# Decode attention: the probabilities of two token steps as one set of 64 weight columns

## The chip, the cores and the metric

The kernel runs on one core of a Trainium2 chip. The metric is device time in microseconds (us) for one launch, as the median of three runs. Beside these runs there is one profiled execution, from which all times of single instructions, waits and transfers come.

The core has five engines, each working through its own list of instructions in order: PE (TensorE, matrix products; its weight loads are listed apart as PEld), DVE (VectorE), ACT (ScalarE), POOL (GpSimd) and SP (SyncE, which here only issues transfers). Engines wait for each other on semaphores. Transfers between device memory and the core's memory are carried by 16 DMA engines.

## The reference

One decode step (one new token for each of four sequences) of a transformer block with sliding-window attention over a cache, and then a gated MLP:

```python
x = A_x                                        # (4, 1, 576)
q = (layernorm(x) @ wq)                        # 32 heads of 128
k, v = last 4096 rows of k_cache, v_cache      # 16 heads of 128; each serves two query heads
p = softmax(q @ k.T * 128 ** -0.5)
h = x + (p @ v) @ wo
g = layernorm(h) @ W_gate
out = h + (g * (g > 0) * (layernorm(h) @ W_up)) @ W_down
```

The caches hold 16384 rows for each head, of which the window takes the last 4096. Keys and values in the window come to 4 sequences x 16 heads x 4096 x 128 bfloat16, for each of the two.

## The kernel before

**Work units.** Four key heads of one sequence form a quad: 128 partitions hold the 4096 rows of four heads (32 partitions for each head, 128 rows in each). There are 16 quads (`NQUAD`), four for each sequence, each with 4 MB of keys and 4 MB of values.

**Transfers.** SP issues all big transfers in one list (line 254 and the lambdas that it calls, L223 for keys, L228 for values, L242 to L254 for the other weights). The order is wq, K0, K1, V0, K2, V1, K3 and so on, V15, then wo, W_gate, W_up and W_down. Keys and values go round four slots of one buffer (`pool`). A transfer into a slot waits until the slot's last user is done: after keys this is the last of the four transposes of the quad (`TR`), after values the quad's last value product (`PV`). SP takes its list strictly in order. W_down waits for `ATTN`, the output projection of attention, since it overwrites the place of wo.

**One quad.** DVE transposes the keys in four parts (`tr`, L397) into three buffers; PE multiplies each part by the queries (`qk`, L463 and L465, 32 products of 512 columns, the second of each two with the weights that the first has loaded: `held`); DVE takes the maximum (`rmax`, L400), ACT and POOL bring it across the partitions, DVE makes a bias from it (`fbias`), ACT takes the exponential (L338), and DVE transposes the probabilities (`trp`, L410) into one of four buffers `pT`. PE then multiplies the values by them (`pv`). PE's order is: the key products of quad i, then the value products of quad i - 1 (`VLEAD` = 1).

**Value products.** A partition holds 128 rows of the window, as four quarters of 32 steps. For one quad `pT` holds 32 steps of 32 columns: the probabilities of the four quarters' rows at that step, for eight query heads each. One product takes the 32 columns of a step as weights and 512 moving columns, the values of the four quarters' rows at the same step, side by side. So there are 32 products in a quad, each with a weight load of its own, and they accumulate. Of each output row only the quarter of the columns is wanted whose values belong to the row's own quarter. The products of quad r of a sequence go to partitions 32r to 32r + 31 of one PSUM bank, so that the four quads of a sequence fill it; two banks (`PVB`, 4 and 5) take turns by sequence.

**Own quarter.** When a sequence is complete, `own(b)` on DVE multiplies the bank by a mask of four (`mask4`) into `own_sb` (L413), and sums over the four quarters into `acc` (L416). `ext(b)` on PE gathers the 32 heads by a 0/1 matrix (`gath`). `own` for the first three sequences runs behind the first key transpose of a later quad (i % 4 == 1); the last one runs after the loop, on the way to the output.

**End.** After the last value products come `SUM` (row sums, from `rowsum`, which DVE makes at L433), `EXT`, `NORM` (L438), `OSEL`, `ATTN` (64 products), the second layernorm, `N1` and `N2` (copies of the transposed rows, on ACT and on DVE at L444), the gate products, the up products, `HH`, two transposes (L450), the down products, one for each piece of W_down and output part, and the store.

Of the kernel before, what the change touches and what calls it, by code (L numbers as in the profile page):

```python
# [6 lines left out]
ACT = mybir.ActivationFunctionType  # L7
ALU = mybir.AluOpType
AX = mybir.AxisListType
# [93 lines left out]
def bass_sequential_preLN__sliding_block_cached__glu_gated_reglu__decode_kernel(  # L103
# [12 lines left out]
    with ExitStack() as es:  # L116
# [23 lines left out]
        own_sb = sb("own_sb", [128, 512], FP32)  # L140
        acc = sb("acc", [128, 2, DH], FP32)
        o_bf = sb("o_bf", [H, DH, B], BF16)
        mask4 = sb("mask4", [128, 4], FP32)
        gath = sb("gath", [128, H], FP32)
# [31 lines left out]
        pb += [es.enter_context(nc.psum_tensor(f"pb{i}", [128, 512], FP32))[:, :] for i in range(4, 8)]  # L176
        PVB, OB, TPB = 4, 6, 7
# [94 lines left out]
        def prog_pool(S):  # L272
            g = "gpsimd"
            S.op(g, lambda e: e.memset(eps_c[:, :], EPS), name="EPS")
            S.op(g, lambda e: e.memset(ident_b[:, :], 0.0), name="P0")
            S.op(g, lambda e: e.memset(qz[:, :, :, :, :].rearrange("p a r c m -> p (a r c m)"), 0.0), name="QZ0")
            S.op(g, lambda e: e.affine_select(out=ident_b[:, :], in_=ident_b[:, :], pattern=[[-1, 128]],  # L277
                                              compare_op=ALU.not_equal, fill=1.0, base=0, channel_multiplier=1),
                 deps=["P0"], name="IDB")
            S.op(g, lambda e: e.memset(xnT[:, :, :], 0.0), name="XNZ")  # L280
            S.op(g, lambda e: e.memset(xn4[:, :, :], 0.0), name="XN4Z")
            S.op(g, lambda e: e.memset(ones_f[:, :], 1.0), name="ONES")
            S.op(g, lambda e: e.memset(spread[:, :, :, :], 0.0), name="SP0")
            S.op(g, lambda e: e.memset(hnT[:, :, :], 0.0), name="HNZ")
            S.op(g, lambda e: e.memset(hn4[:, :, :], 0.0), name="HN4Z")
            S.op(g, lambda e: e.memset(ident_f[:, :], 0.0), name="P1")
            S.op(g, lambda e: e.affine_select(out=ident_f[:, :], in_=ident_f[:, :], pattern=[[-1, 128]],
                                              compare_op=ALU.not_equal, fill=1.0, base=0, channel_multiplier=1),
                 deps=["P1"], name="IDF")
            for i in range(NQUAD):  # L290
                deps = [("EMAX", i)]
                S.op(g, lambda e, i=i: e.partition_all_reduce(bcm[:, i % 2, :], pmax[:, i % 2, :], 128, bass_isa.ReduceOp.max),  # L292
                     deps=deps, name=("PAR", i))


        def prog_act(S):
# [9 lines left out]
            S.op(a, lambda e: e.copy(out=xnT[:, :, 0:B], in_=tpv[:, 0:16].rearrange("p (c b) -> p c b", b=B)), deps=["XNZ"], name="D_XNT")  # L306
            for u in range(2):
# [42 lines left out]
            S.op(a, lambda e: e.copy(out=hnT[0:64, 4, 0:B], in_=tpv[0:64, 16:20]), deps=["TP2", "HN4Z"], name="N1")  # L350
            for u in range(2):
# [8 lines left out]
        def prog_dve(S):  # L360
# [7 lines left out]
            def rows_norm(st, dst, src, deps, name):  # L368
# [11 lines left out]
            S.op(v, lambda e: e.tensor_scalar(out=mask[:, 1, :], in0=mask[:, 0, :], scalar1=FAR, scalar2=-FAR, op0=ALU.mult, op1=ALU.add),  # L380
                 deps=["M0"], name="M1")
            S.op(v, lambda e: e.tensor_reduce(out=mask4[:, :], in_=bass.AP(tensor=ident_b, offset=0, ap=[[128, 128], [NHQ, 4], [32, NPB], [1, NHQ]]),
                                              axis=AX.XY, op=ALU.add), name="MASK4")
            S.op(v, lambda e: e.tensor_scalar(out=foe[:, :].rearrange("p (a s x) -> p a s x", s=NS, x=2),
                                              in0=bass.AP(tensor=ident_b, offset=0, ap=[[128, NS], [0, 16], [1, NS], [0, 2]]),
                                              scalar1=FAR, scalar2=-FAR, op0=ALU.mult, op1=ALU.add), name="FOE")
# [25 lines left out]
            def own(b):  # L412
                S.op(v, lambda e: e.tensor_tensor(out=own_sb[:, :].rearrange("p (q d) -> p q d", d=DH), in0=pb[PVB + b % 2].rearrange("p (q d) -> p q d", d=DH),  # L413
                                                  in1=bass.AP(tensor=mask4, offset=0, ap=[[4, 128], [1, 4], [0, DH]]), op=ALU.mult),
                     deps=[("PV", NPB * b + NPB - 1), "MASK4"], name=("OWN", b))
                S.op(v, lambda e: e.tensor_reduce(out=acc[:, b % 2, :], in_=own_sb[:, :].rearrange("p (q d) -> p d q", d=DH), axis=AX.X, op=ALU.add),  # L416
                     deps=[("OWN", b)] + ([("EXT", b - 2)] if b >= 2 else []), name=("ACC", b))

            for i in range(NQUAD):
                for j in range(4):  # L420
                    tr(i, j)
                    if i == 0 and j == 0:
                        S.op(v, lambda e: e.transpose(out=qT[:, :], in_=q_bf[:, :, :].rearrange("p k x -> p (k x)")), deps=["QBF1"], name="D_QT")  # L423
                        S.op(v, lambda e: e.tensor_reduce(out=gath[:, :].rearrange("p (r h) -> p r h", h=NHQ),
                                                          in_=bass.AP(tensor=ident_f, offset=0, ap=[[128, 128], [32, NPB], [1, NHQ], [NHQ, 4]]),
                                                          axis=AX.X, op=ALU.add), deps=["IDF"], name="GATH")
                    if j == 0 and i > NPB and i % NPB == VLEAD:
                        own(i // NPB - 1)
# [4 lines left out]
            S.op(v, lambda e: e.tensor_tensor(out=rowsum[:, :, :].rearrange("p b (m h) -> p (b m) h", h=NHQ),  # L433
                                              in0=bass.AP(tensor=mask, offset=0, ap=[[2 * NHQ, 128], [0, NQUAD], [1, NHQ]]),
                                              in1=bass.AP(tensor=rs1, offset=0, ap=[[NQUAD, 128], [1, NQUAD], [0, NHQ]]), op=ALU.mult), name="RSUM")
            own(B - 1)
# [3 lines left out]
                 deps=["RS", ("EXT", B - 1)], name="NORM")  # L440
# [3 lines left out]
            S.op(v, lambda e: e.tensor_copy(out=hnT[:, 0:4, 0:B], in_=tpv[:, 0:16].rearrange("p (c b) -> p c b", b=B)), deps=["N1", "HN4Z"], name="N2")  # L444
# [11 lines left out]
        def prog_pe(S):  # L456
# [55 lines left out]
            def pv(i):  # L512
                b, r = divmod(i, NPB)
# [3 lines left out]
                if r == 0 and b >= 2:  # L517
                    deps.append(("OWN", b - 2))
                for t_ in range(TQ // 4):
                    last = t_ == TQ // 4 - 1  # L520
                    mm(pb[PVB + b % 2][32 * r:32 * r + 32, :].rearrange("p (q d) -> p q d", q=4), pT[i % NPT][:, 32 * t_:32 * t_ + 32],
                       vv[:, t_, :, :], t_ == 0, last, deps=deps, name=("PV", i) if last else None)
                    deps = []

            def ext(b):
                mm(pb[OB][0:H, b * DH:(b + 1) * DH], gath[:, :], acc[:, b % 2, :], True, True, deps=[("ACC", b), "GATH"], name=("EXT", b))

            for i in range(NQUAD + VLEAD):
# [3 lines left out]
                if i >= VLEAD:  # L532
                    j = i - VLEAD
                    if j % NPB == 0 and j >= NPB:
                        ext(j // NPB - 1)
# [3 lines left out]
            ext(B - 1)  # L539
# [90 lines left out]
```

## Time and profile before

| what | value |
|---|---|
| median of the runs | 379.45 us (379.43 to 379.69, 3 runs) |
| the profiled execution's own time | 379.33 us |
| span in its profile, first to last instruction | 378.0 us |
| busy: PE, DVE, ACT, POOL | 295.9, 206.0, 52.8, 11.6 us |
| read from device memory | 159.58 MB |
| granted TensorE clock, mean | 0.91 of full |

The profile page gives busy time by engine, a strip of the span in 40 slices, the DMA queues with packets and bytes, the chain of work that ended last followed back from the last instruction, and the costliest groups of instructions with what ended the idle time ahead of each. A line such as L463 is that of the helper that records matmuls, so the tile names and shapes tell which product it is (`pb<-pool,probT ... 128x512` are the value products, `sc<-kT,qz` the key products). Other views of the same trace list instructions in order of time, one row for a run of equal ones, and sum engines over chosen windows.

### The profile page before, as it was taken

Reading aid. Unit: us, or ns where it says so; the run is one execution under the profiler, and the core shown is the slowest. Engines: PE = TensorE matmul, PEld = TensorE weight load, DVE = VectorE, ACT = ScalarE, POOL = GpSimd, SP = SyncE. Lnnn points to the kernel's source line nnn. Section 1 sums busy time; section 2 is a strip of 40 time slices with the busy share of each in tenths; the row PEclk is TensorE's granted clock in tenths of the full one; section 3 lists DMA queues with packets and bytes.
Section 4 is the critical chain, followed back from the end, with each engine's and each line's share of the span. In section 5 each row is a group of like instructions: output and inputs, shape, how many; then the busy total and the mean of one; then the engine's idle time right before and its main releaser. Section 6 shows DMA issues by size and latency. Waiting matters only on the chain.

```text
span 378.0 us, 2813 instructions
## 1 busy us (share of the span) xinstructions
PE 295.9 (78%) x1392; PEld 88.3 (23%) x988; DVE 206.0 (54%) x165; ACT 52.8 (14%) x135; POOL 11.6 (3%) x32
## 2 busy tenths in 40 slices
PE   0059299999986989696959996969698969868566
PEld 0011023223131313131312231313122212322113
DVE  1237577595839392938384846565666566131130
ACT  1013402112020202020201120202002100110020
POOL 4100000000000000000000000000000000000000
PEclk9996879999996999898978998989789998989768
DMA  8999999999999999999999999999999999999995
GB/s 333 430 444 433 413 430 442 437 426 419 434 437 437 418 430 440 433 435 416 433 440 430 432 423 437 433 433 418 433 440 433 428 423 437 426 437 431 407 422 219
DMA packets 6651, 159.76 MB, mean 423 GB/s; under 512 B 744, under 2 KB 880, under 8 KB 1776
## 3 DMA queue, kind: packets, MB, share of 16 engines
q1 hardware_dynamic: 6632, 159.59, 98.6%
q8 instruction: 9, 0.15, 0.2%
q10 hardware_dynamic: 8, 0.00, 0.0%
q14 instruction: 2, 0.02, 0.0%
HBM read 159.58 MB, written 0.00 MB: 422 GB/s over the span
## 4 chain that ended last, share of the span: by engine, by line
DMA 66%; DVE 20%; PE 10%; ACT 2%; SPq 1%; issue 0%; POOL 0%; DVEq 0%
DMA pool<-in_A_k_cache_dram 52%; DVE kT L397 18%; DMA pool<-in_A_v_cache_dram 8%; DMA pool<-in_B_W_down_dram 7%; PE sc L463 4%; PE sc L465 4%; PE pb L463 2%; DVE probT L410 1%; DVE rmx L400 1%; ACT P L338 1%; SPq L254 0%; DVE o_bf L438 0%; ACT L338 0%; ACT qz L327 0%; DVE qT L423 0%
## 5 line engine op out<-in xcount | busy, mean ns | idle before, releaser
L397 DVE STREAM_TRANSPOSE kT<-pool 128x2048 f32<-128x2048 f32 x64 | 142.7, 2281 | 38.4 <-DMA pool<-in_A_k_cache_dram 37.1
L463 PE MATMUL sc<-kT,qz 128*128 128x512 bf16 x256 | 110.7, 432 | 41.2 <-DVE kT L397 41.0
L463 PE MATMUL pb<-pool,probT 128*32 128x512 bf16 (+2 forms) x584 | 120.5, 374 | 4.5 <-DVE probT L450 2.3
L465 PE MATMUL sc<-kT,qz 128*128 128x512 bf16 x256 | 110.2, 431 | 0.0
L463 PEld LDWEIGHTS pb<-pool,probT 128*32 128x32 bf16 (+1 forms) x584 | 52.8, 97 | 74.1 <-issue 13.1
L463 PEld LDWEIGHTS sc<-kT,qz 128*128 128x128 bf16 x256 | 26.7, 104 | 151.8 <-issue 74.6
L400 DVE TENSOR_REDUCE rmx<-sc 128x1 f32<-128x1024 f32 x16 | 19.6, 1224 | 38.9 <-PE sc L465 38.9
L333 ACT ACTIVATE pmax<-mask,rmx 128x8 f32<-128x8 f32 x16 | 4.8, 300 | 236.6 <-DVE rmx L400 236.6
L410 DVE STREAM_TRANSPOSE probT<-P 128x1024 bf16<-128x1024 bf16 x16 | 19.9, 1245 | 20.7 <-ACT P L338 20.7
L338 ACT ACTIVATE P<-sc,bias 128x1024 bf16<-128x1024 f32 x16 | 17.8, 1114 | 13.3 <-DVE bias L405 13.3
L327 ACT COPY qz<-qrep 32x128 bf16<-32x128 bf16 x64 | 18.8, 294 | 0.6
L475 PE MATMUL pb<-ident_b,xn_bf 4*128 4x4 bf16 (+1 forms) x5 | 0.4, 180 | 18.8 <-DVE xn_bf L370 18.8
L292 POOL PARTITION_ALL_REDUCE bcm<-pmax x16 | 5.9, 367 | 297.1 <-ACT pmax L333 297.1
L403 DVE SCALAR_TENSOR_TENSOR t<-bcm,mask 128x8 f32<-128x8 f32 x16 | 2.7, 167 | 13.3 <-POOL bcm L292 13.3
L463 PE MATMUL sc<-pool,oX 128*4 128x288 bf16 x32 | 9.0, 314 | 0.4 <-ACT oX L347 0.4
L465 PE MATMUL sc<-pool,oX 128*4 128x288 bf16 x32 | 9.0, 313 | 0.0
L413 DVE TENSOR_TENSOR own_sb<-pb,mask 128x512 f32<-128x512 f32 x4 | 2.6, 662 | 10.2 <-PE pb L463 10.2
L374 DVE TENSOR_REDUCE sel<-ident_b 128x128 bf16<-128x512 bf16 x1 | 1.0, 1010 | 12.8 <-POOL ident_b L277 12.8
L446 DVE TENSOR_TENSOR P<-pb,P 128x396 bf16<-128x396 f32 x1 | 0.6, 574 | 13.2 <-PE pb L463 13.2
L463 PE MATMUL sc<-col,foe 4*128 4x512 bf16 x16 | 6.4, 398 | 0.7 <-ACT qrep L313 0.7
L441 DVE TENSOR_TENSOR h_row<-sc,x_bf 4x576 f32<-4x576 f32 x1 | 0.7, 746 | 10.3 <-PE sc L465 10.3
L465 PE MATMUL sc<-col,foe 4*128 4x512 bf16 x16 | 6.2, 390 | 0.0
(95 smaller groups left out, 73.4 us busy)
## 6 DMA issues: line engine op xcount, KB each, us to landing
pool<-in_A_k_cache_dram SPq DMA_DIRECT2D x16, 4096.0 KB, 29.5
pool<-in_A_v_cache_dram SPq DMA_DIRECT2D x16, 4096.0 KB, 29.3
pool<-in_A_wo_dram SPq DMA_DIRECT2D x1, 4608.0 KB, 21.3
pool<-in_B_W_gate_dram SPq DMA_DIRECT2D x1, 4608.0 KB, 22.8
pool<-in_B_W_up_dram SPq DMA_DIRECT2D x1, 4608.0 KB, 25.5
pool<-in_A_wq_dram SPq DMA_DIRECT2D x1, 4096.0 KB, 13.0
pool<-in_B_W_down_dram SPq DMA_DIRECT2D x2, 1152.0 KB, 19.4
pool<-in_B_W_down_dram SPq DMA_DIRECT2D x1, 1008.0 KB, 22.5
```

The source lines that it names most:

```text
L292: S.op(g, lambda e, i=i: e.partition_all_reduce(bcm[:, i % 2, :], pmax[:, i % 2, :], 128, bass_isa.ReduceOp.max), deps=deps, name=("PAR", i))
L327: S.op(a, lambda e, src=src, dst=dst: e.copy(out=dst, in_=src), deps=deps, name=("QZ", i) if g == 3 else None, signal=g == 3)
L333: S.op(a, lambda e, i=i: e.activation(out=pmax[:, i % 2, :], in_=mask[:, 1, :], func=ACT.Identity, bias=rmx[:, i % 2:i % 2 + 1], scale=1.0 ...
L338: S.op(a, lambda e, i=i: e.activation(out=Pb[:, (i % 2) * 1024:(i % 2 + 1) * 1024], in_=sc[:, (i % 2) * 1024:(i % 2 + 1) * 1024], func=ACT ...
L374: S.op(v, lambda e: e.tensor_reduce(out=sel[:, :, :], in_=bass.AP(tensor=ident_b, offset=0, ap=[[128, 128], [0, 4], [1, 32], [32, 4]]), ax ...
L397: S.op(v, lambda e: e.transpose(out=dst, in_=src), deps=deps, name=("TR", f))
L400: S.op(v, lambda e: e.tensor_reduce(out=rmx[:, i % 2:i % 2 + 1], in_=sc[:, (i % 2) * 1024:(i % 2 + 1) * 1024], axis=AX.X, op=ALU.max), dep ...
L403: S.op(v, lambda e: e.scalar_tensor_tensor(out=t8[:, :], in0=bcm[:, i % 2, :], scalar=-SCALE, in1=mask[:, 0, :], op0=ALU.mult, op1=ALU.mul ...
L410: S.op(v, lambda e: e.transpose(out=pT[i % NPT], in_=Pb[:, (i % 2) * 1024:(i % 2 + 1) * 1024]), deps=[("EXP", i)] + ([("PV", i - NPT)] if ...
L413: S.op(v, lambda e: e.tensor_tensor(out=own_sb[:, :].rearrange("p (q d) -> p q d", d=DH), in0=pb[PVB + b % 2].rearrange("p (q d) -> p q d" ...
L463: return e.matmul(o, lhsT=l, rhs=r, start=start, stop=stop, skip_group_check=skip)
L465: return e.add_instruction(mybir.InstMatmult(name=nc.get_next_instruction_name(), start_tensor_calc=start, stop_tensor_calc=stop, bass_ski ...
```

## The change

The value products of two neighbouring token steps share one set of weights. Weights are now 64 columns (steps t and t + 1), loaded once; the values of step t are multiplied into one bank and those of step t + 1, with the held weights, into the other. Each quad so fills 64 partitions of both banks, and two quads, not four, complete a window w. Of each output row one eighth is wanted: the own quarter, and the own step's bank. The two banks are one tensor `val` of 1024 columns, and there is no second copy of it: the first product of the next window waits for `OWN` of the last.

`own` now takes 1024 columns with a mask of eight, and runs eight times instead of four; `ext` gathers in two halves, accumulated into the same bank. Four small operations change engine: `M1` and `FOE` from DVE to ACT (in the prologue, L380 and L384 before), `RSUM` from DVE to POOL (L433 before), `N2` from DVE to ACT (L444 before). A clearing of `gath` (`G0`) is added on POOL's prologue.

```diff
--- before.py
+++ after.py
@@ -137,11 +137,11 @@
         oX = sb("oX", [128, EO, B], BF16)
-        own_sb = sb("own_sb", [128, 512], FP32)
+        own_sb = sb("own_sb", [128, 1024], FP32)
         acc = sb("acc", [128, 2, DH], FP32)
         o_bf = sb("o_bf", [H, DH, B], BF16)
-        mask4 = sb("mask4", [128, 4], FP32)
-        gath = sb("gath", [128, H], FP32)
+        mask8 = sb("mask8", [128, 8], FP32)
+        gath = sb("gath", [128, 2, H], FP32)
         qrep = sb("qrep", [128, 4, H * B], BF16)
@@ -173,8 +173,10 @@
         pb = [sc[:, i * 512:(i + 1) * 512] for i in range(4)]
-        pb += [es.enter_context(nc.psum_tensor(f"pb{i}", [128, 512], FP32))[:, :] for i in range(4, 8)]
-        PVB, OB, TPB = 4, 6, 7
+        val = es.enter_context(nc.psum_tensor("val", [128, 1024], FP32))
+        pb += [val[:, i * 512:(i + 1) * 512] for i in range(2)]
+        pb += [es.enter_context(nc.psum_tensor(f"pb{i}", [128, 512], FP32))[:, :] for i in range(6, 8)]
+        OB, TPB = 6, 7
         QB = (5, 6)
@@ -277,6 +279,7 @@
                  deps=["P0"], name="IDB")
+            S.op(g, lambda e: e.memset(gath[:, :, :], 0.0), name="G0")
             S.op(g, lambda e: e.memset(xnT[:, :, :], 0.0), name="XNZ")
@@ -291,6 +294,9 @@
                      deps=deps, name=("PAR", i))
+            S.op(g, lambda e: e.tensor_tensor(out=rowsum[:, :, :].rearrange("p b (m h) -> p (b m) h", h=NHQ),
+                                              in0=bass.AP(tensor=mask, offset=0, ap=[[2 * NHQ, 128], [0, NQUAD], [1, NHQ]]),
+                                              in1=bass.AP(tensor=rs1, offset=0, ap=[[NQUAD, 128], [1, NQUAD], [0, NHQ]]), op=ALU.mult), deps=[("EXP", NQUAD - 1)], name="RSUM")
 
@@ -304,6 +310,10 @@
             S.op(a, lambda e: e.copy(out=xnT[:, :, 0:B], in_=tpv[:, 0:16].rearrange("p (c b) -> p c b", b=B)), deps=["XNZ"], name="D_XNT")
+            S.op(a, lambda e: e.activation(out=foe[:, :].rearrange("p (a s x) -> p a s x", s=NS, x=2),
+                                           in_=bass.AP(tensor=ident_b, offset=0, ap=[[128, NS], [0, 16], [1, NS], [0, 2]]),
+                                           func=ACT.Copy, scale=FAR, bias=-FAR), name="FOE")
+            S.op(a, lambda e: e.activation(out=mask[:, 1, :], in_=mask[:, 0, :], func=ACT.Copy, scale=FAR, bias=-FAR), deps=["M0"], name="M1")
             for u in range(2):
@@ -348,6 +358,7 @@
             S.op(a, lambda e: e.copy(out=hnT[0:64, 4, 0:B], in_=tpv[0:64, 16:20]), deps=["TP2", "HN4Z"], name="N1")
+            S.op(a, lambda e: e.copy(out=hnT[:, 0:4, 0:B], in_=tpv[:, 0:16].rearrange("p (c b) -> p c b", b=B)), name="N2")
             for u in range(2):
@@ -377,13 +388,8 @@
                                               axis=AX.X, op=ALU.add), name="M0")
-            S.op(v, lambda e: e.tensor_scalar(out=mask[:, 1, :], in0=mask[:, 0, :], scalar1=FAR, scalar2=-FAR, op0=ALU.mult, op1=ALU.add),
-                 deps=["M0"], name="M1")
-            S.op(v, lambda e: e.tensor_reduce(out=mask4[:, :], in_=bass.AP(tensor=ident_b, offset=0, ap=[[128, 128], [NHQ, 4], [32, NPB], [1, NHQ]]),
-                                              axis=AX.XY, op=ALU.add), name="MASK4")
-            S.op(v, lambda e: e.tensor_scalar(out=foe[:, :].rearrange("p (a s x) -> p a s x", s=NS, x=2),
-                                              in0=bass.AP(tensor=ident_b, offset=0, ap=[[128, NS], [0, 16], [1, NS], [0, 2]]),
-                                              scalar1=FAR, scalar2=-FAR, op0=ALU.mult, op1=ALU.add), name="FOE")
+            S.op(v, lambda e: e.tensor_reduce(out=mask8[:, :], in_=bass.AP(tensor=ident_b, offset=0, ap=[[128, 128], [NHQ, 8], [64, 2], [1, NHQ]]),
+                                              axis=AX.XY, op=ALU.add), name="MASK8")
             rows_norm(st1, xn_bf, x_bf, ["A_STD"], "XN")
@@ -409,39 +415,35 @@
                      deps=[("EXP", i)] + ([("PV", i - NPT)] if i >= NPT else []), name=("TRP", i))
-            def own(b):
-                S.op(v, lambda e: e.tensor_tensor(out=own_sb[:, :].rearrange("p (q d) -> p q d", d=DH), in0=pb[PVB + b % 2].rearrange("p (q d) -> p q d", d=DH),
-                                                  in1=bass.AP(tensor=mask4, offset=0, ap=[[4, 128], [1, 4], [0, DH]]), op=ALU.mult),
-                     deps=[("PV", NPB * b + NPB - 1), "MASK4"], name=("OWN", b))
-                S.op(v, lambda e: e.tensor_reduce(out=acc[:, b % 2, :], in_=own_sb[:, :].rearrange("p (q d) -> p d q", d=DH), axis=AX.X, op=ALU.add),
-                     deps=[("OWN", b)] + ([("EXT", b - 2)] if b >= 2 else []), name=("ACC", b))
+            def own(w):
+                S.op(v, lambda e: e.tensor_tensor(out=own_sb[:, :].rearrange("p (x d) -> p x d", d=DH), in0=val[:, :].rearrange("p (x d) -> p x d", d=DH),
+                                                  in1=bass.AP(tensor=mask8, offset=0, ap=[[8, 128], [1, 8], [0, DH]]), op=ALU.mult),
+                     deps=[("PV", 2 * w + 1), "MASK8"], name=("OWN", w))
+                S.op(v, lambda e: e.tensor_reduce(out=acc[:, w % 2, :], in_=own_sb[:, :].rearrange("p (x d) -> p d x", d=DH), axis=AX.X, op=ALU.add),
+                     deps=[("OWN", w)] + ([("EXT", w - 2)] if w >= 2 else []), name=("ACC", w))
 
                         S.op(v, lambda e: e.transpose(out=qT[:, :], in_=q_bf[:, :, :].rearrange("p k x -> p (k x)")), deps=["QBF1"], name="D_QT")
-                        S.op(v, lambda e: e.tensor_reduce(out=gath[:, :].rearrange("p (r h) -> p r h", h=NHQ),
-                                                          in_=bass.AP(tensor=ident_f, offset=0, ap=[[128, 128], [32, NPB], [1, NHQ], [NHQ, 4]]),
-                                                          axis=AX.X, op=ALU.add), deps=["IDF"], name="GATH")
-                    if j == 0 and i > NPB and i % NPB == VLEAD:
-                        own(i // NPB - 1)
+                        S.op(v, lambda e: e.tensor_reduce(out=bass.AP(tensor=gath, offset=0, ap=[[2 * H, 128], [H + 16, 2], [NHQ, 2], [1, NHQ]]),
+                                                          in_=bass.AP(tensor=ident_f, offset=0, ap=[[128, 128], [0, 2], [64, 2], [1, NHQ], [NHQ, 8]]),
+                                                          axis=AX.X, op=ALU.add), deps=["IDF", "G0"], name="GATH")
+                    if j == 0 and i > 1 and i % 2 == VLEAD:
+                        own(i // 2 - 1)
                 rmax(i)
 
-            S.op(v, lambda e: e.tensor_tensor(out=rowsum[:, :, :].rearrange("p b (m h) -> p (b m) h", h=NHQ),
-                                              in0=bass.AP(tensor=mask, offset=0, ap=[[2 * NHQ, 128], [0, NQUAD], [1, NHQ]]),
-                                              in1=bass.AP(tensor=rs1, offset=0, ap=[[NQUAD, 128], [1, NQUAD], [0, NHQ]]), op=ALU.mult), name="RSUM")
-            own(B - 1)
+            own(NQUAD // 2 - 1)
             S.op(v, lambda e: e.reciprocal(out=rs_sb[:, :], in_=pb[TPB][0:H, 0:B]), deps=["SUM"], name="RS")
                                               in1=bass.AP(tensor=rs_sb, offset=0, ap=[[B, H], [1, B], [0, DH]]), op=ALU.mult),
-                 deps=["RS", ("EXT", B - 1)], name="NORM")
+                 deps=["RS", ("EXT", NQUAD // 2 - 1)], name="NORM")
             S.op(v, lambda e: e.tensor_tensor(out=h_row[:, :], in0=attn, in1=x_bf[:, :], op=ALU.add), deps=["ATTN", land("x")], name="H")
             rows_norm(st2, hn_row, h_row, ["A_STD2"], "HN")
-            S.op(v, lambda e: e.tensor_copy(out=hnT[:, 0:4, 0:B], in_=tpv[:, 0:16].rearrange("p (c b) -> p c b", b=B)), deps=["N1", "HN4Z"], name="N2")
             for k, (f0, f1) in enumerate(CUTS):
@@ -510,20 +512,22 @@
             def pv(i):
-                b, r = divmod(i, NPB)
+                w, r = divmod(i, 2)
                 x0 = at[("V", i)]
                 deps = [("TRP", i), land(("V", i))]
-                if r == 0 and b >= 2:
-                    deps.append(("OWN", b - 2))
+                if r == 0 and w >= 1:
+                    deps.append(("OWN", w - 1))
                 for t_ in range(TQ // 4):
+                    k = t_ % 2
                     last = t_ == TQ // 4 - 1
-                    mm(pb[PVB + b % 2][32 * r:32 * r + 32, :].rearrange("p (q d) -> p q d", q=4), pT[i % NPT][:, 32 * t_:32 * t_ + 32],
-                       vv[:, t_, :, :], t_ == 0, last, deps=deps, name=("PV", i) if last else None)
+                    mm(val[64 * r:64 * r + 64, 512 * k:512 * k + 512].rearrange("p (q d) -> p q d", q=4), pT[i % NPT][:, 32 * (t_ - k):32 * (t_ - k) + 64],
+                       vv[:, t_, :, :], t_ < 2, t_ >= TQ // 4 - 2, deps=deps, name=("PV", i) if last else None, held=k == 1)
                     deps = []
 
-            def ext(b):
-                mm(pb[OB][0:H, b * DH:(b + 1) * DH], gath[:, :], acc[:, b % 2, :], True, True, deps=[("ACC", b), "GATH"], name=("EXT", b))
+            def ext(w):
+                b, k = divmod(w, 2)
+                mm(pb[OB][0:H, b * DH:(b + 1) * DH], gath[:, k, :], acc[:, w % 2, :], k == 0, k == 1, deps=[("ACC", w), "GATH"], name=("EXT", w))
 
@@ -531,12 +535,12 @@
                     j = i - VLEAD
-                    if j % NPB == 0 and j >= NPB:
-                        ext(j // NPB - 1)
+                    if j % 2 == 0 and j >= 2:
+                        ext(j // 2 - 1)
                     pv(j)
                 mm(pb[TPB][0:H, b:b + 1], rowsum[:, b, :], ones_f[:, 0:1], True, True, deps=["RSUM", "ONES"] if b == 0 else [], name="SUM" if b == B - 1 else None)
-            ext(B - 1)
+            ext(NQUAD // 2 - 1)
 
```

## The prediction, made before the change was run

> **What bounds the kernel now.** I read the page first: busy time, the strip and the DMA queues.
>
> ```profile
> span 378.0 us, 2813 instructions
> ...
> PE 295.9 (78%) x1392; PEld 88.3 (23%) x988; DVE 206.0 (54%) x165; ACT 52.8 (14%) x135; POOL 11.6 (3%) x32
> ...
> DMA  8999999999999999999999999999999999999995
> ...
> q1 hardware_dynamic: 6632, 159.59, 98.6%
> q8 instruction: 9, 0.15, 0.2%
> ```
>
> The 16 DMA engines are at nine tenths or more in every slice but the first and last, and the data queue takes 98.6% of their span: the kernel moves 159.6 MB and cannot end before they are through. No compute engine passes 78%. Then I read one quad in the timeline, for how far compute stays behind the transfers.
>
> ```profile
> 132.57 8.89 DVE L397 STREAM_TRANSPOSE kT<-pool 128x2048 f32<-128x2048 f32 x4 [1.00 <-DMA pool<-in_A_k_cache_dram]
> ...
> 135.63 0.39 PE L465 MATMUL sc<-kT,qz 128*128 128x512 bf16 x1
> ...
> 135.85 0.39 PE L463 MATMUL sc<-kT,qz 128*128 128x512 bf16 x1
> ...
> 143.42 7.08 PE L463 MATMUL pb<-pool,probT 128*32 128x512 bf16 x32
> ...
> 147.21 1.25 DVE L410 STREAM_TRANSPOSE probT<-P 128x1024 bf16<-128x1024 bf16 x1 [1.27 <-ACT P L338]
> ...
> 152.00 8.89 DVE L397 STREAM_TRANSPOSE kT<-pool 128x2048 f32<-128x2048 f32 x4 [3.54 <-DMA pool<-in_A_k_cache_dram]
> ```
>
> Quads follow each other every 19.43 us (152.00 - 132.57). DVE's chain for one, first transpose to last, takes 15.9 us (147.21 + 1.25 - 132.57); then DVE waits 3.54 us for keys. From the chain of waits:
>
> ```profile
> 141.49 29.95 DMA pool<-in_A_k_cache_dram
> ...
> 258.06 29.92 DMA pool<-in_A_k_cache_dram
> ```
>
> A key transfer lands 29.95 us after its slot came free. From 171.44 (141.49 + 29.95) to 287.98 twelve transfers land, 9.71 us each. So when one is issued, about 20 us (29.95 - 9.71) of other transfers are still ahead of it: a slot may come free that much later before a DMA engine runs dry.
>
> **How the end comes about.**
>
> ```profile
> 318.72 7.08 PE L463 MATMUL pb<-pool,probT 128*32 128x512 bf16 x32
> ...
> 323.68 0.25 DVE L433 TENSOR_TENSOR rowsum<-mask,rs 128x128 f32<-128x128 f32 x1
> ...
> 326.97 6.42 PE L463 MATMUL pb<-pool,probT 128*32 128x512 bf16 x29 [1.17 <-DMA pool<-in_A_v_cache_dram]
> ...
> 334.08 0.69 DVE L413 TENSOR_TENSOR own_sb<-pb,mask 128x512 f32<-128x512 f32 x1 [10.15 <-PE pb L463]
> ...
> 334.80 1.02 DVE L416 TENSOR_REDUCE acc<-own_sb 128x128 f32<-128x512 f32 x1
> ```
>
> ```profile
> 347.98 8.89 SPq L254 DMA_DIRECT2D pool<-in_B_W_down_dram  x7
> ...
> 351.60 0.17 DVE L444 COPY hnT<-pb 128x16 bf16<-128x16 bf16 x1 [0.69 <-ACT hnT L350]
> ...
> 355.48 0.70 PE L463 MATMUL pb<-h_row,ident_f 4*4 4x320 f32 x4
> 359.64 0.52 PE L463 MATMUL pb<-pool,hnT 128*32 128x396 bf16 x4 [3.46 <-DMA pool<-in_B_W_up_dram]
> ...
> 367.81 5.00 PE L463 MATMUL pb<-pool,probT 128*4 128x320 bf16 x46 [2.32 <-DVE probT L450]
> ...
> 373.41 0.98 PE L463 MATMUL pb<-pool,probT 128*4 128x320 bf16 x12 [0.60 <-DMA pool<-in_B_W_down_dram]
> ...
> 374.78 1.37 PE L463 MATMUL pb<-pool,probT 128*4 128x320 bf16 x14 [0.40 <-DMA pool<-in_B_W_down_dram]
> ...
> 376.20 0.41 ACT L357 CAST out_sb<-pb 4x320 bf16<-4x320 f32 x1 [9.98 <-PE pb L463]
> ```
>
> The chain of the last quad waits for V15 (1.17 us), for W_up (3.46) and for pieces of W_down (0.60, 0.40); after the last piece some 2 us remain. W_down is issued at 347.98, while W_up still comes until 359.64, so there are over 11 us in the queue. The end is the landing of W_down's last piece. What makes that late is seen in narrow windows:
>
> ```profile
> 374.00:374.50 0.50, 0.38 (x6) 0.04 (x1) 0.00 (x0) 0.00 (x0) 0.00 (x0) 1.00 0.19 71
> 374.50:375.50 1.00, 0.70 (x8) 0.33 (x8) 0.00 (x0) 0.00 (x0) 0.00 (x0) 1.00 0.06 23
> ```
>
> The last column but one is the DMA share. 0.19 is three engines of 16, and 0.06 is one alone: for about 0.9 us, to nearly 375.5, fifteen DMA engines are done and one works off its part.
>
> **Part by part.** *Transfers of data*: unchanged, 0.
>
> *PE's value products.* 512 products of 512 columns stay; every second weight load goes, 256 in all. PE goes at 221 ns a product with a load each (7.08 / 32), against 220 between key products (135.85 - 135.63), where every second load is held. So the loads were hidden, and I count 0. A product with 64 weight columns is not in the trace; the neighbours, 32 and 128 columns, go at 221 and 220 ns, so I take the same.
>
> *DVE's own parts.* The rows, by line:
>
> ```profile
> L400 DVE TENSOR_REDUCE rmx<-sc 128x1 f32<-128x1024 f32 x16 | 19.6, 1224 | 38.9 <-PE sc L465 38.9
> ...
> L405 DVE TENSOR_REDUCE bias<-t 128x1 f32<-128x8 f32 x16 | 2.6, 161 | 0.5
> ...
> L413 DVE TENSOR_TENSOR own_sb<-pb,mask 128x512 f32<-128x512 f32 x4 | 2.6, 662 | 10.2 <-PE pb L463 10.2
> ...
> L416 DVE TENSOR_REDUCE acc<-own_sb 128x128 f32<-128x512 f32 x4 | 4.1, 1035 | 0.1
> ```
>
> From 8 to 1024 elements a reduction grows by 1.06 us, or 0.53 for 512. So `OWN` goes to 0.66 + 0.53 = 1.2 and `ACC` to 1.04 + 0.53 = 1.57: 2.8 us a pair. Plain doubling is the upper end, 1.32 + 2.07 = 3.4; the old pair, 1.7, the lower. I take 2.8, since the reductions show a fixed part. Eight pairs in place of four add 15.6 us of DVE (22.4 - 6.8), but not to the time: in every second quad the chain becomes 15.9 + 2.8 = 18.7, still under 19.43, and the other quads wait 3.5 us as before. Three key transposes are queued behind the pair, so the key slot comes free 2.8 us later, out of 20 us of queue.
>
> *The added wait*: window w + 1's first product waits for `OWN` w. `OWN` stands in DVE's list ahead of three key transposes whose key products PE does before that product. So PE waits on the transposes anyway: 0. `OWN` itself waits for the quad's products two back, which end at 150.5 (143.42 + 7.08), while its place comes at 152.00 + 2.2: no wait.
>
> *Moved operations.* `M1`, `FOE` and `G0` lie in the prologue, before DVE's wait for the first keys:
>
> ```profile
> 24.77 2.31 DVE L397 STREAM_TRANSPOSE kT<-pool 128x2048 f32<-128x2048 f32 x1 [6.00 <-DMA pool<-in_A_k_cache_dram]
> ```
>
> Whatever the two take on ACT and the one on POOL, up to these 6.00 us, is covered: 0. `RSUM` (0.25 on DVE) goes to POOL, which is then free; it has until the last product ends, some 10 us. `N2` (0.17) changes engine: 0 within 0.1.
>
> *The last quad.* One pair now stands behind its first key transpose, so PV14 starts and ends 2.8 later, at 328.6. PV15 then follows PV14 and not V15: 1.65 late (2.8 less the 1.17 wait). The last pair takes 2.8, not 1.74 (334.08 to 335.82): 1.06 more. So `ATTN` is 2.7 us late, 3.9 with plain doubling. W_down is issued at 350.7 with 9 us still queued: no gap. The up products still wait for W_up, since 2.7 is under 3.46: 0. With 3.9 they start 0.4 late; that is the cover's end.
>
> *The instruction stream.* The page's q8 queue brings PE's instructions: nine fetches, 0.15 MB, 16 KB each. 2380 matmuls and loads (1392 + 988) over nine is one in some 260.
>
> ```profile
> q8 instruction: 1, 0.02, 2.8%
> ```
>
> That is the window 363 to 365.5: the ninth fetch is there, with 2.8% of 16 engines' 2.5 us, 1.1 us of one engine. No other comes between it and the straggler above. PE's count up to it, and between the eighth and the ninth:
>
> ```profile
> 0.00:364.12 364.12, 287.19 (x1305) 83.99 (x912) 202.43 (x159) 50.27 (x132) 11.59 (x32) 0.91 1.00 428
> ```
>
> ```profile
> 342.23:364.12 21.89, 15.04 (x162) 3.79 (x68) 2.64 (x7) 0.93 (x5) 0.00 (x0) 0.79 0.98 415
> ```
>
> The ninth comes at 2217 instructions, the eighth at 1987. The new PE program has 2380 - 256 + 16 (four more gathers, two passes with a load each) = 2140: it ends before a ninth, and its eighth moves to the place of the old ninth. If the straggler is the engine that served the ninth fetch on top of an earlier one, the end comes 0.9 us sooner. Which engine serves a fetch no view prints; the landing events of single engines, of which no view is a list, agree that the ninth fell on the engine of the first, the other seven on seven others. So I take the 0.9.
>
> On this the Trainium skill, page "Runtime: NRT & Kernel Launch", section "Instruction fetch mechanics", says that instructions come in 16 KiB blocks of 256, which the trace agrees with, and that the cost of a block is mostly hidden. By that the sum would be 0; the straggler speaks against it here.
>
> **Sum.** 0 + 0 - 0.9 from 379.33: 378.4. The median stands 0.12 above the profiled execution, so for the median 378.55; I say 378.5.
>
> **Rivals.**
>
> *No straggler to win* (379.1 to 379.6): the eighth fetch, now in the tail, takes the same engine, or a second engine is as late for another cause. For it, from the window 110 to 310:
>
> ```profile
> q8 instruction: 5, 0.08, 0.2%
> ```
>
> Five fetches lie there, and the steps stay 9.71, so most fetches move no last landing. By the page's rule, too, a fetch is hidden.
>
> *The eighth fetch falls on an engine already late*: done at 374.5, plus the 1.1 of a fetch and up to half a us of turning between the two queues (an estimate: half a packet), that is 375.6 to 376.1, against 375.5: 379.4 to 380.0.
>
> *The own pair takes the end* (slower). A pair of x makes `ATTN` late by (x - 1.17) + (x - 1.74). At x = 3.2 this is W_up's 3.46; beyond, the end moves by 2 for each us of x, after the 0.9 is used up. From x = 4.0 it is slower by over 0.76; at 4.6 about 381. Against it: doubling gives only 3.4.
> The Trainium skill, page "TensorEngine Tiling (Array Packing)", section "PSUM Bottleneck", warns that tiling speeds the products and not the emptying of PSUM; here it is the emptying that grows.
>
> *PE becomes the engine that bounds*: products with 64 columns at twice 221 ns. A quad's 34 key products (7.5) and 32 at 442 (14.1) make 21.6, over 19.43: 2.2 x 16 = 35 us slower. It decides from about 0.37 us a product. Against it: the 32 and 128 column rows.
>
> **How the numbers follow.** A measurement of this kernel tells about 0.2%, 0.76 us, from no change: under 378.69 is faster. Forecast, 378.2 to 378.9: 0.60, of it 0.48 below 378.69. No straggler to win: 0.20, same. Eighth on a late engine: 0.05, of it 0.02 slower. Own pair: 0.07, slower. PE: 0.03, slower. More gained than 0.9, if the engines next in line are relieved too (three were still busy at 374): 0.05, faster. Faster 0.53, same 0.35, slower 0.12. The range 378.0 to 379.8 leaves out the last two rivals and the ends of others, some 0.15.
>
> **What would show it.** Right: q8 with eight fetches; no window of 0.9 us with one DMA engine alone near the end; own pairs near 2.8 us; keys' steps 9.71 with DVE still waiting for keys; the up products still waiting for W_up. Wrong: a wait of DVE or PE at a window's change, PE's products above 0.3 us, or a last W_down piece landing where it did with eight fetches.

## The result, and the profile after

The changed kernel takes 378.21 us (median of 8 runs, 378.03 to 378.69) against 379.35 for the kernel before (8 runs, 379.26 to 379.69): a ratio of 0.9971, 95% interval 0.9960 to 0.9982. That is 1.1 us faster; 378.5 was predicted. Its profiled execution took 378.24 us, with a span of 376.9.

The page of the changed kernel, busy time and DMA queues:

```profile
span 376.9 us, 2583 instructions
...
PE 298.2 (79%) x1400; PEld 68.7 (18%) x740; DVE 222.8 (59%) x169; ACT 53.0 (14%) x138; POOL 12.1 (3%) x34
...
q1 hardware_dynamic: 6632, 159.59, 98.8%
q8 instruction: 8, 0.13, 0.1%
```

1400 + 740 are the 2140 matmuls and loads that were counted ahead, with eight fetches and not nine. DVE is busy for 17 us more, and the kernel is still faster. The data are the same 159.59 MB.

The end in narrow windows of the changed kernel (the last but one column is the DMA share):

```profile
374.00:374.50 0.50, 0.50 (x10) 0.35 (x7) 0.00 (x0) 0.00 (x0) 0.00 (x0) 1.00 0.05 16
374.50:375.50 1.00, 0.57 (x8) 0.17 (x3) 0.38 (x1) 0.39 (x1) 0.00 (x0) 1.00 0.00 0
```

One DMA engine is alone for at most half a us, and from 374.5 on nothing moves; before, one engine went on alone to nearly 375.5.

The middle, from the chain of waits of the changed kernel:

```profile
163.67 26.84 DMA pool<-in_A_k_cache_dram
...
280.23 26.83 DMA pool<-in_A_k_cache_dram
```

Keys land at 190.51 and 307.06, twelve transfers apart: 9.71 us each, as before. From issue to landing it is now 26.8 us and not 29.9: the slot comes free 3.1 us later. That comes out of the queue's depth, and the landings stay where they were.

The last quad in the timeline of the changed kernel:

```profile
307.08 2.31 DVE L403 STREAM_TRANSPOSE kT<-pool 128x2048 f32<-128x2048 f32 x1 [3.31 <-DMA pool<-in_A_k_cache_dram]
309.32 1.19 DVE L419 TENSOR_TENSOR own_sb<-val,mask 128x1024 f32<-128x1024 f32 x1
310.54 1.90 DVE L422 TENSOR_REDUCE acc<-own_sb 128x128 f32<-128x1024 f32 x1
```

DVE still waits 3.31 us for keys, after a quad without an own pair. The pair takes 3.1 us.

```profile
352.83 3.69 SPq L256 DMA_DIRECT2D pool<-in_B_W_down_dram  x7
```

```profile
360.72 0.52 PE L465 MATMUL pb<-pool,hnT 128*32 128x396 bf16 x4
...
368.70 6.37 PE L465 MATMUL val<-pool,probT 128*4 128x320 bf16 x72 [2.98 <-DVE probT L452]
```

`ATTN` releases W_down at 352.83, 4.85 us later than before (347.98). The up products no longer wait for W_up, and all 72 down products run in one row with no wait for W_down. So in this execution PE's chain ends last, and behind `ATTN` no wait for a transfer is left in it.

The changed kernel was profiled a second time (the first repeat among the last experiments, 378.12 us), and there the end is different:

```profile
350.33 6.21 SPq L256 DMA_DIRECT2D pool<-in_B_W_down_dram  x7
```

```profile
359.33 0.35 PE L465 MATMUL pb<-pool,hnT 128*32 128x396 bf16 x4 [0.75 <-DMA pool<-in_B_W_up_dram]
...
373.57 1.37 PE L465 MATMUL val<-pool,probT 128*4 128x320 bf16 x14 [0.40 <-DMA pool<-in_B_W_down_dram]
```

W_down is released 2.35 us later than before, the up products wait for W_up, and the last down products wait for W_down. The two executions differ by only 0.12 us (378.24 and 378.12), so the chain and the transfers end almost together.

### The profile page after: what moved, and what is told of

Same layout as the page of the kernel before. It is cut to its first block, busy times and chain, and to the rows that moved or that the text cites. A ratio compares the mean times of both kernels' runs of the same rounds, so it can differ in the third digit from the quotient of the medians.

```text
span 376.9 us, 2583 instructions
## 1 busy us (share of the span) xinstructions
PE 298.2 (79%) x1400; PEld 68.7 (18%) x740; DVE 222.8 (59%) x169; ACT 53.0 (14%) x138; POOL 12.1 (3%) x34
## 3 DMA queue, kind: packets, MB, share of 16 engines
q1 hardware_dynamic: 6632, 159.59, 98.8%
## 4 chain that ended last, share of the span: by engine, by line
DMA 48%; DVE 29%; PE 18%; ACT 3%; issue 1%; SPq 0%; POOL 0%; DVEq 0%
DMA pool<-in_A_k_cache_dram 48%; DVE kT L403 19%; PE sc L467 6%; PE sc L465 6%; DVE acc L422 4%; PE val L465 4%; DVE own_sb L419 2%; PE val L467 2%; DVE probT L416 1%; DVE rmx L406 1%; ACT P L348 1%; PE pb L465 1%; ACT P L366 0%; DVE o_bf L441 0%; ACT L348 0%
## 5 line engine op out<-in xcount | busy, mean ns | idle before, releaser
L465 PE MATMUL val<-pool,probT 128*64 128x512 bf16 (+2 forms) x328 | 103.0, 370 | 3.0 <-DVE probT L452 3.0
L467 PE MATMUL val<-pool,probT 128*64 128x512 bf16 x256 | 96.2, 379 | 0.0
L465 PEld LDWEIGHTS val<-pool,probT 128*64 128x64 bf16 (+1 forms) x328 | 32.1, 106 | 86.1 <-issue 81.8
L422 DVE TENSOR_REDUCE acc<-own_sb 128x128 f32<-128x1024 f32 x8 | 15.2, 1899 | 0.3
L419 DVE TENSOR_TENSOR own_sb<-val,mask 128x1024 f32<-128x1024 f32 x8 | 9.5, 1192 | 8.3 <-PE val L467 8.3
L465 PE MATMUL sc<-pool,oX 128*4 128x288 bf16 x32 | 10.1, 340 | 0.4 <-ACT oX L357 0.4
L467 PE MATMUL sc<-pool,oX 128*4 128x288 bf16 x32 | 10.0, 340 | 0.0
L444 DVE TENSOR_TENSOR h_row<-sc,x_bf 4x576 f32<-4x576 f32 x1 | 0.7, 746 | 11.7 <-PE sc L467 11.7
L465 PE MATMUL sc<-col,foe 4*128 4x512 bf16 x16 | 6.4, 398 | 0.7 <-ACT qrep L323 0.7
## 6 DMA issues: line engine op xcount, KB each, us to landing
pool<-in_A_k_cache_dram SPq DMA_DIRECT2D x16, 4096.0 KB, 26.8
```

The source lines that it names most:

```text
L422: S.op(v, lambda e: e.tensor_reduce(out=acc[:, w % 2, :], in_=own_sb[:, :].rearrange("p (x d) -> p d x", d=DH), axis=AX.X, op=ALU.add), de ...
L465: return e.matmul(o, lhsT=l, rhs=r, start=start, stop=stop, skip_group_check=skip)
L467: return e.add_instruction(mybir.InstMatmult(name=nc.get_next_instruction_name(), start_tensor_calc=start, stop_tensor_calc=stop, bass_ski ...
```

## The experiments

The theory going in: the ninth fetch of PE's instructions put one DMA engine behind all the others, and a shorter PE program does without it. The rivals: the weight loads' own time, the operations moved off DVE, or the rest of the change gained it. The ratios are to the kernel before on the same chip.

**Half the weight loads, nothing else.** (The edits are abridged, here and below.)

```diff
-    mm(pb[PVB + b % 2][32 * r:32 * r + 32, :]..., pT[i % NPT][:, 32 * t_:32 * t_ + 32], ...)
+    mm(pb[PVB + b % 2][32 * r:32 * r + 32, :]..., pT[i % NPT][:, 32 * (t_ - t_ % 2):32 * (t_ - t_ % 2) + 32], ..., held=t_ % 2 == 1)
```

> The kernel before, with one thing changed: every second value product keeps the weights of the product ahead of it, so that 256 weight loads of 32 columns go and nothing else (the odd steps are then multiplied by the even steps' probabilities, so the output leaves those out). Theory (the ninth instruction fetch on PE's queue makes one DMA engine the last, and goes when PE's program is shorter than 2217 matmuls and loads): eight fetches, 378.2 to 378.7 us against 379.35. Rival (the gain comes from the other parts: own pairs, moved operations, two banks): 379.2 to 379.5, also with eight fetches.

Measured: 378.76 us, 0.9978 (0.9968 to 0.9988). Its page, and the window near the end:

```profile
PE 294.6 (78%) x1392; PEld 63.7 (17%) x732; DVE 205.8 (55%) x165; ACT 52.8 (14%) x135; POOL 11.6 (3%) x32
...
q8 instruction: 8, 0.13, 0.1%
```

```profile
374.50:375.00 0.50, 0.50 (x8) 0.20 (x4) 0.00 (x0) 0.00 (x0) 0.00 (x0) 1.00 0.06 23
375.00:375.50 0.50, 0.49 (x7) 0.17 (x6) 0.00 (x0) 0.00 (x0) 0.00 (x0) 1.00 0.00 0
```

The gain comes with the loads, without own pairs of 1024 columns and without the moved operations. It is 0.06 above the range that the theory gave. In this execution one engine is alone to 375.0; the repeat below has none so late.

**The changed kernel, its PE program made as long as before.**

```diff
                     pv(j)
+                    if j < NQUAD - 1:
+                        for _ in range(8):
+                            mm(pb[TPB][0:4, 256:260], ident_b[0:4, 0:4], ident_b[0:4, 0:4], True, True)
```

> The changed kernel, with eight tiny products (4 x 4, into an unused corner of a bank) behind the value products of each of 15 quads: 240 more matmuls and loads, 2380 in all, as before. Theory (ninth fetch): nine fetches, the ninth in the tail, 379.0 to 379.5 us. Rival (the gain comes from the weight loads or other parts, not from the number of instructions): 378.0 to 378.5.

**The same with `range(2)`.**

> The same with two tiny products a quad: 60 more matmuls and loads, 2200 in all, under the 2217 at which the ninth fetch came. Theory: eight fetches, 378.0 to 378.5 us, as the changed kernel. Rival (the tiny products themselves cost time, a quarter of what eight a quad cost): 378.4 to 378.6 if eight a quad cost 0.9.

Measured: with eight tiny products a quad 379.46 us, 0.9999 (0.9990 to 1.0008); with two 378.16, 0.9963 (0.9951 to 0.9976). The page and the end, first with eight:

```profile
PE 299.5 (79%) x1520; PEld 71.7 (19%) x860; DVE 222.6 (59%) x169; ACT 53.1 (14%) x138; POOL 12.1 (3%) x34
...
q8 instruction: 9, 0.15, 0.2%
```

```profile
374.00:374.50 0.50, 0.44 (x7) 0.09 (x1) 0.00 (x0) 0.00 (x0) 0.00 (x0) 1.00 0.07 25
374.50:375.00 0.50, 0.17 (x4) 0.14 (x6) 0.00 (x0) 0.00 (x0) 0.00 (x0) 1.00 0.07 28
375.00:375.50 0.50, 0.50 (x8) 0.19 (x4) 0.00 (x0) 0.00 (x0) 0.00 (x0) 1.00 0.06 23
```

and with two:

```profile
PE 297.7 (79%) x1430; PEld 69.7 (18%) x770; DVE 222.7 (59%) x169; ACT 53.1 (14%) x138; POOL 12.1 (3%) x34
...
q8 instruction: 8, 0.13, 0.1%
```

```profile
374.00:374.50 0.50, 0.49 (x8) 0.15 (x6) 0.00 (x0) 0.00 (x0) 0.00 (x0) 1.00 0.06 21
374.50:375.00 0.50, 0.50 (x6) 0.09 (x3) 0.00 (x0) 0.00 (x0) 0.00 (x0) 1.00 0.00 0
```

This decides it. Both have the whole change in them. At 2200 matmuls and loads the gain is all there, at 2380 it is all gone, and the ninth fetch and the lone engine to 375.5 are back. So neither the weight loads' own time nor the rest of the change is the gain. The tiny products themselves cost nothing that can be measured: 60 of their instructions show no loss here, and 240 of them in the kernel before, further down, give 1.0003.

**The moved operations alone.**

```diff
-            S.op(v, ... name="M1") ... "FOE" ... "RSUM" ... "N2"
+            S.op(a, ... name="FOE") ... "M1" ... "N2"
+            S.op(g, ... name="G0") ... "RSUM"
```

> The kernel before with the moved operations alone: M1, FOE and N2 on ACT, RSUM on POOL, the clearing G0 added; value products, loads and own pairs as before. Theory (number of PE instructions): nine fetches, 379.2 to 379.7 us. Rival (moving them off DVE is what gained): 378.2 to 378.6.

Measured: 379.50 us, 0.9998 (0.9990 to 1.0007), with nine fetches and the lone engine:

```profile
375.00:375.50 0.50, 0.50 (x8) 0.16 (x3) 0.00 (x0) 0.00 (x0) 0.00 (x0) 1.00 0.05 18
```

The moves alone gain nothing.

**One load for a quad, and ten fetches.** The first holds the first step's weights through all 32 products; the second puts the eight tiny products into the kernel before.

```diff
-    ..., pT[i % NPT][:, 32 * t_:32 * t_ + 32], ...)
+    ..., pT[i % NPT][:, 0:32], ..., held=t_ > 0)
```

> The kernel before with one weight load for the 32 value products of a quad (all steps are multiplied by the first step's probabilities, so the output leaves the other 31 out): 1884 matmuls and loads, under the 1987 at which the eighth fetch came, so seven fetches. Theory (a fetch costs time only where it falls on an engine that is late from an earlier one): as with eight fetches, 378.2 to 378.9 us. Rival (every fetch left out is worth some 0.8 us): 377.4 to 378.0.

> The kernel before with eight tiny products behind the value products of each of 15 quads: 2620 matmuls and loads, so ten fetches, the tenth some 150 instructions ahead of the end. Theory (the ninth and tenth fall on two engines that are late already, each by about as much): 379.4 to 380.0 us, since one more engine is late and not the same one twice more. Rival (every fetch costs 0.8 to 1.0): 380.2 to 380.6.

Measured: one load 378.55 us, 0.9978 (0.9969 to 0.9986); ten fetches 379.74, 1.0003 (0.9994 to 1.0012). One load:

```profile
q8 instruction: 7, 0.11, 0.1%
```

```profile
374.00:374.50 0.50, 0.50 (x8) 0.25 (x7) 0.00 (x0) 0.00 (x0) 0.00 (x0) 1.00 0.22 78
374.50:375.00 0.50, 0.49 (x8) 0.10 (x6) 0.00 (x0) 0.00 (x0) 0.00 (x0) 1.00 0.01 2
```

Ten fetches:

```profile
q8 instruction: 10, 0.16, 0.2%
```

```profile
374.00:374.50 0.50, 0.50 (x7) 0.25 (x3) 0.00 (x0) 0.00 (x0) 0.00 (x0) 0.50 0.15 55
374.50:375.00 0.50, 0.50 (x5) 0.09 (x4) 0.00 (x0) 0.00 (x0) 0.00 (x0) 0.50 0.14 55
```

With seven fetches the ratio is that of eight (0.9978 both), with ten it is not told from nine. So a fetch has no price of its own: from eight to nine it is 1.3 us (378.16 to 379.46, on one chip), else too little to measure. With ten, the share of 0.14 says two engines: a second one is as late as the first, which moves the end little.

With one load, three of the eleven runs took 379.27 to 379.85 us, as long as the kernel before; none of these was profiled, so their cause is open.

**Which engine a fetch delays.** The engine of a fetch is in no view. But each big transfer comes in sixteen parts, and the kept traces hold the time at which each part landed. From one transfer to the next the distances between the sixteen mostly stay the same to some hundredths of a us. After a PE fetch one part is 1.4 to 1.7 us further back, and stays there. (The two fetches of another queue, q14, near 80 and 100 us, do the same by 0.7 to 1.1.) The table gives the place of the part that the last fetch hits, counted from the earliest, and how far the last part of the last piece of W_down lands behind the last but one:

| run | PE fetches | place before, after | last behind last but one, us |
|---|---|---|---|
| kernel before | 9 | 10, 16 | 0.9 |
| changed, eight tiny products a quad | 9 | 13, 16 | 1.4 |
| moves alone | 9 | 10, 16 | 1.1 |
| ten fetches (the tenth) | 10 | 9, 15 | 0.1 |
| changed kernel | 8 | 5, 13 | 0.1 |
| changed, two tiny products a quad | 8 | 1, 8 | 0.3 |
| one load | 7 | 3, 8 | 0.2 |

With seven or eight fetches each falls on a part that none has hit before; the last one moves an early part into the field and nothing ends later. The ninth falls on a part that is far back already and makes it the last. Followed from transfer to transfer, that is the part of the first fetch in the kernel before, in the padded one and in the one with ten fetches; with the moves alone the parts stand too close together to tell. With ten, the tenth's part comes to lie beside the ninth's, and the last part comes 0.1 us later than in the kernel before (375.91 against 375.81). In the first execution of the loads alone, the lone part to 375.0 is one that no PE fetch hit: it was the last from the first key transfers on. So the lateness is shown part by part; that the parts are the sixteen engines is inferred from their number and from the shares above.

**The own pair behind the fourth key transpose.**

```diff
-                    if j == 0 and i > 1 and i % 2 == VLEAD:
+                    if j == 3 and i > 1 and i % 2 == VLEAD:
```

> The changed kernel, with the own pair behind the fourth key transpose of the quad and not behind the first. In the changed kernel's tail the down products run with no wait for W_down, so PE's chain ends about when the transfers do. Theory (both end together, DMA engines a few tenths ahead): the attention projection some 2 us earlier, waits for W_down again, 377.9 to 378.3 us. Rival (the chain of the last quad is what sets the end, the transfers have slack): 377.0 to 377.7.

Measured: 378.10 us, 0.9964 (0.9951 to 0.9976).

```profile
350.24 6.35 SPq L256 DMA_DIRECT2D pool<-in_B_W_down_dram  x7
```

```profile
373.58 1.37 PE L465 MATMUL val<-pool,probT 128*4 128x320 bf16 x14 [0.34 <-DMA pool<-in_B_W_down_dram]
```

W_down is issued 2.6 us sooner than in the first execution of the changed kernel (350.24 against 352.83), the last down products wait for W_down, and the time is the same as that of the lightly padded kernel beside it (378.16). So an earlier chain gains nothing: the transfers hold the end then. That the edit is what makes the chain earlier is not shown, since the second execution of the unedited kernel has 350.33 and waits for W_down in the same way.

**Every own pair twice.**

```diff
+                S.op(v, ... out=own_sb ..., name=("OWN0", w))
+                S.op(v, ... out=acc[:, w % 2, :] ..., name=("ACC0", w))
                 S.op(v, ... out=own_sb ..., deps=[("ACC0", w)], name=("OWN", w))
```

> The changed kernel with every own pair done twice, one behind the other: 3.1 us more of DVE in eight places. Theory (covered in the middle, since a pair of quads has 7 us of slack on DVE, but not at the end, where two pairs lie on the chain of the last quad and its cover is used up): keys' steps stay 9.71 us, and the end moves by about 2 x 3.1, to 383.5 to 385. Rival (the cover at the end still holds): 378.0 to 378.7. Other rival (the middle loses too): 390 and more.

Measured: 389.91 us, 1.0276 (1.0260 to 1.0291). The theory was too low by five; what came is the second rival, that the middle loses too (390 and more), within 0.1. From its chain of waits, the first transposes of every second quad:

```profile
77.03 2.19 DVE kT L403
...
116.14 2.19 DVE kT L403
...
154.51 2.19 DVE kT L403
...
194.11 2.19 DVE kT L403
```

Two quads take 39.1, 38.4 and 39.6 us here, 39.0 in the mean, against 38.84 at the pace of the keys (4 x 9.71). After the very first keys DVE never waits for keys again, and the last quad's transposes begin at 311.08 and not at 307.08. Two chains of 15.9 and a pair of 6.2 would be 38.0 and still fit; the last us is DVE's longer wait for the key products in quads with a pair, here in one without and in the next, with one:

```profile
149.59 1.22 DVE L406 TENSOR_REDUCE rmx<-sc 128x1 f32<-128x1024 f32 x1 [2.07 <-PE sc L472]
...
173.42 1.23 DVE L406 TENSOR_REDUCE rmx<-sc 128x1 f32<-128x1024 f32 x1 [3.88 <-PE sc L472]
```

**Loads and moves together, and two repeats on one chip.**

> The kernel before with both: half the weight loads (odd steps multiplied by the even steps' probabilities) and the moved operations, the own pairs as before. Open is why half the loads alone gave 0.7 us and the whole change 1.1 to 1.3. Theory (the moved operations shift the other instruction queue's two fetches apart, so they fall on engines that are not late): 378.0 to 378.4 us. Rival (the rest comes from the two banks and own pairs, or is the spread between chips): as with the loads alone on this chip, 378.6 to 378.9.

> The changed kernel as it is, on the same chip as the runs beside it, for comparison: 378.0 to 378.4 us by both.

> The kernel before with half the weight loads alone, as in the first experiment, on the same chip: 378.6 to 378.9 us if the difference to the changed kernel is one of the kernels; 378.0 to 378.4 if it was chance.

Measured: both 378.29 us, 0.9970 (0.9959 to 0.9981); the changed kernel 378.53, 0.9972 (0.9961 to 0.9984); the loads alone 378.55, 0.9977 (0.9966 to 0.9987). The first is inside its theory's range; the changed kernel is 0.13 above the 378.0 to 378.4 expected, and the loads alone fall between their two ranges. The three intervals overlap, and single runs of one kernel lie 0.6 us and more apart. That the moves help the loads along is neither shown nor excluded.

The profiled execution of the repeated loads alone took 378.88 us, as that of the first (378.89), but for another reason:

```profile
374.00:374.50 0.50, 0.50 (x9) 0.35 (x5) 0.00 (x0) 0.00 (x0) 0.00 (x0) 0.50 0.15 53
374.50:375.00 0.50, 0.50 (x8) 0.29 (x5) 0.00 (x0) 0.00 (x0) 0.00 (x0) 0.50 0.00 0
```

Nothing moves after 374.5, but PE's clock (the last column but two) was granted at 0.50, and the down products ended last. Without the lone engine PE's chain is close behind, and a slow clock then shows in the time.

## Why the prediction was right

- *What bounds the kernel* held: the queue's share is 98.8% against 98.6% and the steps stay at 9.71 us.
- *The instruction stream* held in cause and count: 2140, eight fetches, no lone engine. The ninth fetch fell on a part that the first had put back, as the prediction had it. Its size was 0.9; the kernel pair gives 1.1, the pair of padded kernels 1.3. The 0.9 is the lead of the last part over the next one in the one execution read. The ones next in line were less late too: before, the last but one part of W_down landed 0.7 us behind the middle of the sixteen, and now the very last lands 0.4 us behind it; the forecast had kept this as a case with 0.05. Why they differ from execution to execution is open.
- *PE's value products* were counted at 0. Two rows of the changed kernel, seven products apart:

```profile
323.38 0.38 PE L467 MATMUL val<-pool,probT 128*64 128x512 bf16 x1
...
324.89 0.38 PE L465 MATMUL val<-pool,probT 128*64 128x512 bf16 x1
```

 They give 216 ns a product, 5 less than before, 0.2 us a quad, off the path. The rival of a slow 64-column product falls. The 5 ns go with the loads: with 32 columns and half the loads, the first experiment's last 32 value products start 216 ns apart too (327.45 to 334.14). That rival's price was a little too high: a quad has 32 key products and not 34, so it would have cost 28 us and not 35.
- *DVE's own parts* were mis-sized: 2.8 was taken, 3.1 came.

```profile
L422 DVE TENSOR_REDUCE acc<-own_sb 128x128 f32<-128x1024 f32 x8 | 15.2, 1899 | 0.3
L419 DVE TENSOR_TENSOR own_sb<-val,mask 128x1024 f32<-128x1024 f32 x8 | 9.5, 1192 | 8.3 <-PE val L467 8.3
```

 `OWN` met its 1.2. `ACC` took 1.90 and not 1.57. The step from 8 to 1024 elements was read off a reduction to one output, and this one has 128 outputs and reads across rows; doubling the old `ACC`, of the same kind (2.07), was the nearer row. Which of the two differences counts was not tested.
- *The last quad*: 2.7 us late were forecast. In the second execution of the changed kernel 2.35 came, and the up products waited for W_up as forecast (0.75). In the first 4.85 came, beyond even the 3.9 of plain doubling, and they did not wait. The larger pairs make 0.6 of that. Most of the rest goes with PE's clock, first in the last key products, here in the first and in the second execution:

```profile
309.00:320.20 11.20, 8.63 (x21) 1.45 (x11) 10.01 (x6) 0.00 (x0) 0.00 (x0) 0.54 0.99 424
```

```profile
309.00:320.20 11.20, 8.28 (x29) 1.54 (x15) 10.05 (x6) 0.00 (x0) 0.00 (x0) 0.85 0.99 427
```

 and then in `ATTN`, of the first execution and of the kernel before:

```profile
342.20:352.80 10.60, 10.58 (x64) 3.17 (x32) 0.00 (x0) 1.17 (x1) 0.00 (x0) 0.75 0.95 408
```

```profile
338.60:347.96 9.36, 9.33 (x64) 2.95 (x32) 0.00 (x0) 1.17 (x1) 0.00 (x0) 0.85 1.03 439
```

 The sum had every product at its old pace. At 0.75 `ATTN`'s 64 products took 10.6 us, at 0.85 they took 9.4. Why the clock differs between two executions of one kernel no run shows. The lateness cost next to nothing, as the two executions are 0.12 us apart: the forecast let the cover end at W_up's 3.46, but the waits for W_down behind it (0.60 and 0.40 before) were cover as well.
- *The own pair as the bound*: the point of decision was put at the end, at a pair of 4.0. The doubled pair of 6.2 gave 11.7 us over the changed kernel, much more than 2 for each us (6.2 for the 3.1 added), since it used up DVE's slack in the middle as well: 4.0 us by the last quad.
- *The rule that a fetch is mostly hidden* (the Trainium skill, page "Runtime: NRT & Kernel Launch", section "Instruction fetch mechanics") holds here for seven against eight fetches (0.9978 both). It does not hold for the ninth, which costs 1.3 us by way of the transfers; there the measurement decides.

## What to carry to other kernels

Where the transfers fill the DMA engines to the end, the time is that of the slowest of the 16; look at the DMA share in windows of half a us near the end, and if one engine goes on alone, ask what else it carried. Count instructions against the fetches on the page: a shorter program can win although no instruction removed was on the path, and a longer one can lose. And profile a kernel twice before reading a wait of a us or two as its own: here two executions of one kernel, 0.12 us apart in time, had different waits at the end, and clocks of 0.54 and 0.85 in the same stretch.

## What the runs showed of the hardware

- PE's instructions come in blocks over the same DMA engines as the data: nine fetches of 16 KB for 2380 matmuls and loads, eight for 2140 and 2200, seven for 1884, ten for 2620.
- Each fetch put one of the sixteen parts of all later transfers back by 1.4 to 1.7 us for good, while the queue stayed full.
- A single fetch of 16 KB, one part in ten thousand of the data, moved the end of the kernel by 1.3 us or by too little to measure, by where it fell.
- A product of 512 columns with 64 weight columns, every second load held, went at 216 ns, as with 32 columns and every second load held; with 32 columns and a load each it was 221.
